# A fused attention and two-layer MoE kernel: a new order for the whole first phase, masks on VectorE, small steps on ScalarE, half-size weight checks

## The chip, the core and the metric

The kernel runs on one core of a Trainium2 chip. Its engines work from queues of their own, each in its order: TensorE (PE, with PEld for its weight loads), VectorE (DVE), ScalarE (ACT), GpSimd (POOL) and SyncE (SP), which issues the DMAs. The metric is the device time of one execution in microseconds (us).

## The reference

`x` is the output of a linear attention with a decaying state, for 4 batches, 8 heads, 768 positions and 48 features; then two dense layers follow, each on 3072 tokens of 384 features.

```python
for t in range(S):                                            # attention
    state = alpha[:, :, t, :, None] * state + np.einsum('bhd,bhe->bhde', k[:, :, t], v[:, :, t])
    y[:, :, t] = np.einsum('bhd,bhde->bhe', q[:, :, t], state)

h = x @ w_in                                                  # 384 -> 1024
e = np.exp(h - np.max(h, axis=-1, keepdims=True))
solu = h * (e / (np.sum(e, axis=-1, keepdims=True) + 1e-09))
mu = np.mean(solu, axis=-1, keepdims=True)
var = np.mean((solu - mu) ** 2, axis=-1, keepdims=True)
x = ((solu - mu) / np.sqrt(var + 1e-06) * g_ln) @ w_out       # 1024 -> 384

h = x @ w_in2                                                 # 384 -> 2048
out = (h * np.cos(h)) @ w_out2                                # 2048 -> 384
```

The weights arrive as 64-bit floats.

## The kernel before

**First phase.** The tokens are cut into 24 tiles of 128 (6 to a batch). For each tile the kernel runs an attention part and a first-layer part.

Attention of tile i: two scans over the decays with a floor and a reciprocal between them (`scan_to`, `total_floor`, `total_inverse`, `scan_from`; `S1` to `S4` in the list, all DVE), the scaling of keys and queries (`keys`, `queries`: `KR`, `QP` on POOL or `KV`, `QV` on DVE), a transposition of the keys (`TR`, PE) and its copy (`KT`, ACT), the scores (`SC`, PE, into PSUM tile `pa`), the causal mask into `am`, the state's product, addition and decay (`ST` PE, `SD` DVE, `SP` POOL or `SV` DVE), the values (`VA`, PE, into `px`), and their split into a high part `xh` (`XH`, ACT) and a low part `xl` (`XL`, DVE). The mask is made in one of two ways: `MV`, one DVE multiplication from PSUM, or `ME` and `MP`, a copy on ACT and a multiplication in place on POOL. The list has 7 tiles of the first kind and 17 of the second.

First layer of tile s: three products `HD s.0` to `HD s.2` (`hidden`, 18 matmuls of 512 columns in all, PE), the row maximum (`SM`, DVE), the exponential (`EX`, ACT), the guarded inverse (`O1`, `O2`), the product (`O3`) and the mean (`O4`, all DVE), the squares (`SQ`, ACT), three one-column steps on POOL (`PW`, `spread`), the normalisation (`NO`, ACT), its transposition in two halves (`TU`, PE), split into high and low parts (`TH` ACT, `TL` DVE). Every two tiles, three `project` groups of 24 matmuls (`PR`) give the columns of `x2T`, copied by ACT (`PX`). `ph`, the output of `hidden`, has one buffer, so that `HD s+1` waits for `O3` of tile s.

**Weights.** Each 64-bit block is read as pairs of integers and turned into a 32-bit float: a shift (`C1`, L206) and a sign step (`C2`, L210) on DVE, the low word on ACT (`CA`), the addition on POOL (`CD`) or DVE (`CV`). The 10 blocks of the first layer (`i0` to `i5`, `o0` to `o3`) are split into high and low parts (`WH` on ACT; `WL` on POOL or `WV` on DVE); the 16 blocks of the second layer are stored to a scratch in HBM (`WS`) and read again at the start of the second phase. `conv_load` (`CL`) has one buffer `raw` and three `top`.

**Order.** Every engine runs its instructions as they are issued, and they are issued in the order of one list, `PLAN`. Its head and tail are tables written out by hand (`START`, `END`); between them `_plan` makes one round for each tile from a template. A word of it is an operation and its tile or block: `HD4.0` is the first product of tile 4 (the fifth tile).

**Second phase.** 6 blocks of 512 tokens times 16 chunks of 128 hidden features make 96 slots. In slot t, PE runs `h2` of the chunk after and `out_mm` of the chunk two before (18 matmuls of 512 columns), ACT and DVE compute `h cos h` in between (`turns` L589, `residue` L595 and L596, `cosine` L602, `product` L607, `split_high` L612, `split_low` L617). At chunks 8 to 10 of a block, POOL makes a low part of the next block's input (`x2l`, L574). At the end of a block `out_end` copies and stores its three outputs. 42 slots from the 17th on also check the inputs: 18 blocks of `alpha` (`check`: POOL, then DVE L649) and 24 weight blocks of 128 x 768 (`check_weights`: a shift L657 and a comparison with a sum L658 on DVE, one buffer `wraw`), taking turns while there are both. A flag from them decides at the end whether a general path runs; it does not here.

Of the kernel before, what the change touches and what calls it, by code (L numbers as in the profile page):

```python
# [64 lines left out]
START = """  # L65
LP0 S10 CL0 S20 LP1 S30 S40 LQ0 CA0 QP0 C10 ID C20 S11 CL1 LQ1 S21 MK LV0 KV0 S31 TR0 C11 KT0 CL3 CD0 SC0 S41
ST0 KR1 CL2 C21 MV0 SD0 LP2 LV1 WH0 TR1 C13 C12 C23 QP1 C22 CA1 KT1 WL0 S12 CD1 VA0 SC1 S22 CL4
ME1 C14 LQ2 SV6 LV2 XH0 MP1 GL ST1 WH1 SD1 XL0 S32 WL1 C24 SP1 SP5 QP2 CA2 CA3 S42 CA4 CL5 LD3 CD3 CV2 CL6
C15 VA1 S13 S23 XH1 XL1 C25 HD0.0 KR2 TR2 SC2 S33 LD4 KT2 S43 ST2 QP3 MV2 WH3 CD4 VA2 WH2 KR3 SD2
TR3 CA5 WH4 SC3 XH2 CV5 C16 WL2 WL3 SP2 S14 C26 KT3 HD0.1 WH5 WL4 WL5 S24 ME3 S34 MP3 HD0.2 XL2  # L70
SM0 LD5 CA6 ST3 S44 QP4 SD3 EX0 VA3 O10 KR4 CL7 TR4 O20 XH3 O30 CD6 O40 XL3 SC4 SQ0 SP3 PW0 ME4 MP4 S15 C17 SV0
NO0 KT4 S25 QP5 C27 S35 HD1.0 CA7 WH6 HD1.1 HD1.2 ST4 LD6 S45 TU0.1 CD7 VA4 TH0.1 KR5 TU0.0 SM1 EX1 SD4 
O11 O21 O31 TR5 SP4 XH4 SC5 O41 S16 CL8 WH7 SQ1 TL0.1 HD2.0 WL6 PW1 ME5 HD2.1 C18 S26 S36 HD2.2 NO1 TU1.0 CA8 XL4 C28
S46 LD7 MP5 TH0.0 SM2 TL0.0 KR6 TH1.0 EX2 TU1.1 VA5 TR6 O12 TH1.1 QP6 XH5 KT6 O22 SC6 CD8 ME6 TL1.0 O32 LD8
S17 CL9 WL7 O42 TL1.1 WH8 XL5 MP6 HD3.0 S27 S37 S47 HD3.1 KR7 ST6 QP7 SD6 C19 S18 HD3.2 VA6 S28 C29 SQ2 S38 QV8
CA9 PW2 XH6 TR7 S48 KT7 LD9 SC7 ST7 SM3 NO2 KR8 SD7 TU2.1 TR8 SD5 ME7 XL6 SC8 EX3 TU2.0 CL10 O13 O23 CV9 KT8
O33 MP7 TH2.1 ST5 C110 VA7 HD4.0 TH2.0 HD4.1 TL2.1 WV8 WH9 O43 XH7 SP7 WV9 SQ3 TL2.0 HD4.2 PW3 LD10 C210 PR0.0 XL7
ST8 S19 MV8 CA10 NO3 S29 SD8 SP8 TU3.1 S39 S110 VA8 CL11 TH3.1 SM4 PX0.0 PR0.1 CD10 TU3.0 S210 EX4 TH3.0
TL3.1 S49 PX0.1 TL3.0 O14 O24 XH8 PR0.2 PX0.2 QP9 CA11 O34 O44 S310 SQ4 KR9 TR9 PW4 C111 KT9 SC9 HD5.0 HD5.1 C211
HD5.2 MV9 NO4 TU4.1 TH4.1 TU4.0 KT5 XL8 CD11 ST9 VA9 CL12 SM5 LD11 EX5 TL4.1 SD9 O15 TH4.0 TL4.0 PR1.0  # L80
S410 O25 KV10 O35 XH9 XL9 QP10 O45 PR1.1 SP9 S111 SQ5 TR10 PW5 SC10 WS10 S211 NO5 QP11 WS11 S311 MV10 S411 PX1.0 PX1.1
KT10 KR11 LD12 CA12 C112 C212 CD12 CL13 HD6.0 HD6.1 HD6.2 SM6 TU5.0 TU5.1 TH5.0 TL5.0 TH5.1 TL5.1 ST10 VA10
LD13 EX6 O16 O26 O36 O46 SD10 SP10 XH10 XL10 SQ6 PW6 PR1.2 PX1.2 PR2.0 PX2.0 PR2.1 PX2.1 TR11 SC11 NO6
"""
# [16 lines left out]


def _plan():

# [3 lines left out]
    start, end = table(START), table(END)  # L110
# [837 lines left out]
```

## Time and profile before

| | |
|---|---|
| median of 3 runs | 796.62 us (793.13 to 798.89) |
| profiled execution | 794.76 us, of which the span is 792.8 us |
| PE busy in the span | 741.8 us (94%) |
| DVE busy | 596.3 us (75%) |
| ACT busy | 404.7 us (51%) |
| POOL busy | 295.7 us (37%) |
| first phase, by the profile | 0 to about 380 us |

Times in the rows are counted from the start of the span. Busy time of PE includes matmuls that overlap. In a timeline, what stands in brackets at the end of a row is how long the engine was idle before it, and what ended that; neighbouring DVE instructions overlap by about 0.1 us.

### The profile page before, as it was taken

Reading aid. Unit: us, or ns where it says so; the run is one execution under the profiler, and the core shown is the slowest. Engines: PE = TensorE matmul, PEld = TensorE weight load, DVE = VectorE, ACT = ScalarE, POOL = GpSimd, SP = SyncE. Lnnn points to the kernel's source line nnn. Section 1 sums busy time; section 2 is a strip of 40 time slices with the busy share of each in tenths; the row PEclk is TensorE's granted clock in tenths of the full one; section 3 lists DMA queues with packets and bytes.
Section 4 is the critical chain, followed back from the end, with each engine's and each line's share of the span. In section 5 each row is a group of like instructions: output and inputs, shape, how many; then the busy total and the mean of one; then the engine's idle time right before and its main releaser. Section 6 shows DMA issues by size and latency. Waiting matters only on the chain.

```text
span 792.8 us, 13293 instructions
## 1 busy us (share of the span) xinstructions
PE 741.8 (94%) x5260; PEld 609.3 (77%) x5260; DVE 596.3 (75%) x937; ACT 404.7 (51%) x645; POOL 295.7 (37%) x229
## 2 busy tenths in 40 slices
PE   6587799999999999999999999999999899999997
PEld 3466588988888778979877787878787678888885
DVE  9998987677777696455567699979989876666664
ACT  3247544465566445556665454444444445545443
POOL 5789744567686732212454125123311100100000
PEclk9779999999999999999999999999999999999999
DMA  8734437556555542111221333243433411001001
GB/s 297 177 94 117 135 78 168 158 143 167 138 156 151 149 96 81 61 38 43 80 87 47 119 133 107 94 159 110 151 104 128 159 41 41 0 1 41 0 1 43
DMA packets 24502, 81.13 MB, mean 102 GB/s; under 512 B 3217, under 2 KB 6545, under 8 KB 24433
## 3 DMA queue, kind: packets, MB, share of 16 engines
q1 hardware_dynamic: 24432, 80.21, 33.6%
q8 instruction: 43, 0.70, 0.4%
q14 instruction: 27, 0.21, 0.1%
HBM read 69.19 MB, written 11.01 MB: 101 GB/s over the span
## 4 chain that ended last, share of the span: by engine, by line
PE 53%; DVE 25%; ACT 7%; DMA 7%; issue 5%; POOL 3%; ACTq 0%; SPq 0%; POOLq 0%; DVEq 0%
PE ph L423 10%; PE o L630 4%; PE h L582 4%; PE h L583 4%; PE h L584 4%; PE o L628 4%; PE o L629 4%; PE po L499 4%; DMA wraw<-w 4%; PE po L500 4%; PE po L501 4%; DVE r L596 3%; DVE r L595 3%; ACT g L602 3%; PE px L361 2%
## 5 line engine op out<-in xcount | busy, mean ns | idle before, releaser
L602 ACT ACTIVATE g<-r,halfpi 128x512 f32<-128x512 f32 x96 | 69.6, 725 | 146.7 <-DVE r L596 146.7
L630 PE MATMUL o<-gl,w2h 128*128 128x512 f32 x288 | 115.5, 401 | 10.0 <-DVE gl L617 9.9
L628 PE MATMUL o<-gh,w2h 128*128 128x512 f32 x288 | 113.8, 395 | 0.0
L582 PE MATMUL h<-x2h,w2h 128*128 128x512 f32 x288 | 113.7, 395 | 0.0
L583 PE MATMUL h<-x2l,w2h 128*128 128x512 f32 x288 | 113.5, 394 | 0.0
L629 PE MATMUL o<-gh,w2l 128*128 128x512 f32 x288 | 113.3, 393 | 0.0
L584 PE MATMUL h<-x2h,w2l 128*128 128x512 f32 x288 | 113.1, 393 | 0.0
L595 DVE SCALAR_TENSOR_TENSOR r<-n,h 128x512 f32<-128x512 int32 x96 | 65.8, 685 | 55.5 <-ACT n L589 55.5
L589 ACT ACTIVATE n<-h,quarter 128x512 int32<-128x512 f32 x96 | 65.7, 684 | 53.3 <-PE h L584 53.1
L607 DVE TENSOR_TENSOR g<-g,h 128x512 f32<-128x512 f32 x96 | 66.0, 688 | 31.3 <-ACT g L602 31.3
L499 PE MATMUL po<-lth,wout_h 128*128 128x256 f32 x288 | 82.4, 286 | 1.4 <-DVE ltl L492 1.0
L500 PE MATMUL po<-ltl,wout_h 128*128 128x256 f32 x288 | 80.7, 280 | 0.5 <-DVE ltl L492 0.5
L501 PE MATMUL po<-lth,wout_l 128*128 128x256 f32 x288 | 80.4, 279 | 0.0
L648 POOL TENSOR_SCALAR lim<-al 128x512 f32<-128x512 f32 x18 | 38.7, 2151 | 102.2 <-DMA al<-alpha 70.0
L630 PEld LDWEIGHTS o<-gl,w2h 128*128 128x128 f32 x288 | 54.0, 188 | 29.4 <-DVE gl L617 17.3
L596 DVE SCALAR_TENSOR_TENSOR r<-n,r 128x512 f32<-128x512 int32 x96 | 71.8, 748 | 3.3
L617 DVE TENSOR_TENSOR gl<-g,gh 128x512 fp32r<-128x512 f32 x96 | 67.6, 706 | 1.5 <-ACT gh L612 1.5
L429 DVE TENSOR_REDUCE c<-ph 128x1 f32<-128x1024 f32 x24 | 29.3, 1222 | 50.5 <-PE ph L423 46.4
L574 POOL TENSOR_TENSOR x2l<-x2T,x2h 128x512 fp32r<-128x512 f32 x15 | 19.4, 1296 | 119.8 <-ACT x2h L570 119.8
L582 PEld LDWEIGHTS h<-x2h,w2h 128*128 128x128 f32 x288 | 54.0, 188 | 12.7
L584 PEld LDWEIGHTS h<-x2h,w2l 128*128 128x128 f32 x288 | 54.1, 188 | 12.6
L629 PEld LDWEIGHTS o<-gh,w2l 128*128 128x128 f32 x288 | 54.0, 188 | 12.6
(116 smaller groups left out, 1605.3 us busy)
## 6 DMA issues: line engine op xcount, KB each, us to landing
raw<-w SPq DMA_DIRECT2D x16, 768.0 KB, 4.5
wraw<-w SPq DMA_DIRECT2D x16, 768.0 KB, 4.3
pk<-pack SPq DMA_DIRECT2D x42, 288.9 KB, 5.3
w2f<-top SPq DMA_DIRECT2D x16, 384.0 KB, 5.2
w2r<-w2f SPq DMA_DIRECT2D x16, 384.0 KB, 3.0
v<-vpack SPq DMA_DIRECT2D x24, 224.0 KB, 5.4
al<-alpha SPq DMA_DIRECT2D x18, 256.0 KB, 4.5
outT<-ob SPq DMA_DIRECT2D x18, 256.0 KB, 2.1
```

The lines of the kernel that those rows point to most:

```text
L499: PE.matmul(po, wout_h[:, k, fs], lh[:, k, :], start=k == 0, stop=False)
L500: PE.matmul(po, wout_h[:, k, fs], ll[:, k, :], start=False, stop=False)
L501: PE.matmul(po, wout_l[:, k, fs], lh[:, k, :], start=False, stop=k == NF1 - 1)
L582: PE.matmul(ph, wh[:, ks], xh[:, k, :], start=k == 0, stop=False)
L583: PE.matmul(ph, wh[:, ks], xl[:, k, :], start=False, stop=False)
L584: PE.matmul(ph, wl[:, ks], xh[:, k, :], start=False, stop=k == KT - 1)
L595: V.scalar_tensor_tensor(out=r, in0=n, scalar=-C1, in1=ph, op0=ALU.mult, op1=ALU.add)
L596: V.scalar_tensor_tensor(out=r, in0=n, scalar=-C2, in1=r, op0=ALU.mult, op1=ALU.add)
L602: A.activation(g, r, AF.Sin, bias=halfpi)
L628: PE.matmul(po, wh[:, fs], gh, start=c == 0, stop=False)
L629: PE.matmul(po, wl[:, fs], gh, start=False, stop=False)
L630: PE.matmul(po, wh[:, fs], gl, start=False, stop=c == NF2 - 1)
```

## The change

`PLAN` is written out as one table for the whole first phase; `START`, `END` and `_plan` are gone. In its words: all 24 masks are `MV` (DVE), and `ME`, `MP` do not exist any more. Keys are on DVE for 11 tiles (4 before), queries for 8 (2 before), the low parts of 5 weight blocks (2 before) and the additions of 8 (4 before). 8 state decays run on ACT (`SA`, four activations each), 8 on POOL, none on DVE. The guard and the mean have ACT versions (`A1` for 18 tiles, `A4` for 15). The three POOL steps of `spread` become one on ACT (`PA`), the power on POOL (`PW`) and one on ACT (`PB`). The memsets of states and constants move from DVE to POOL. `raw` has two buffers and `top` two. The weights are checked in 48 halves of 128 x 384 with two buffers, so that 66 slots hold a check.

```diff
-NWB = (KT * FF1 + NF1 * DM) // WB + NF2
+HB = WB // 2
+NWB = ((KT * FF1 + NF1 * DM) // WB + NF2) * 2
...
+PLAN = """
+LP0 GL CL0 MK LV0 ID LQ0 S10 LP1 S20 S30 S40 CA0 CL1 C10 C20 LV1 CD0 WH0 KV0 LQ1 WV0 TR0 LP2 S11 KT0 ST0 S21 S31 QP0
...
-                raw = cv.tile([128, WB, 2], I32, name=f"raw{name}", tag="raw", bufs=1)
-                tmp = [cv.tile([128, WB], I32, name=f"{t}{name}", tag=t, bufs=n) for t, n in (("top", 3), ("low", 1))]
+                raw = cv.tile([128, WB, 2], I32, name=f"raw{name}", tag="raw")
+                tmp = [cv.tile([128, WB], I32, name=f"{t}{name}", tag=t, bufs=n) for t, n in (("top", 2), ("low", 1))]
...
         def state_decay(i, eng=G):
             if 0 < i % NCH < NCH - 1:
                 P, st = T["P", i], T["st", i]
-                eng.tensor_tensor(st, st, P[:, :, C:C + 1].to_broadcast([128, NP, 96]), ALU.mult)
+                if eng is A:
+                    for p in range(NP):
+                        A.activation(st[:, p, :], st[:, p, :], AF.Copy, scale=P[:, p, C:C + 1])
+                else:
+                    eng.tensor_tensor(st, st, P[:, :, C:C + 1].to_broadcast([128, NP, 96]), ALU.mult)
...
+                A.activation(c[:, 1:2], c[:, 1:2], AF.Identity, bias=guards)
...
+                A.activation(c[:, 3:4], c[:, 3:4], AF.Copy, scale=-1.0 / FF1)
...
+        def variance(i):
+            c = T["c", i]
+            A.activation(c[:, 5:6], c[:, 4:5], AF.Identity, scale=1.0 / FF1, bias=tiny)
+
         def spread(i):
             c = T["c", i]
-            G.tensor_scalar(c[:, 5:6], c[:, 4:5], 1.0 / FF1, 1e-6, ALU.mult, ALU.add)
             G.tensor_tensor(c[:, 6:7], c[:, 5:6], mhalf, ALU.pow)
-            G.tensor_tensor(c[:, 7:8], c[:, 6:7], c[:, 3:4], ALU.mult)
+
+        def offset(i):
+            c = T["c", i]
+            A.activation(c[:, 7:8], c[:, 3:4], AF.Copy, scale=c[:, 6:7])
...
-            raw = pools["q3"].tile([128, WB, 2], I32, name=f"wraw{j}", tag="wraw", bufs=1)
-            y = pools["q3"].tile([128, WB], U32, name=f"wup{j}", tag="wup", bufs=1)
-            SP.dma_start(raw, weight_block(a, j).bitcast(I32).rearrange("p (n two) -> p n two", two=2))
+            raw = pools["q3"].tile([128, HB, 2], I32, name=f"wraw{j}", tag="wraw")
+            y = pools["q3"].tile([128, HB], U32, name=f"wup{j}", tag="wup", bufs=1)
+            src = weight_block(a, j // 2)[:, j % 2 * HB:(j % 2 + 1) * HB]
+            SP.dma_start(raw, src.bitcast(I32).rearrange("p (n two) -> p n two", two=2))
```

**Three places of the order.** On DVE at the start of the program, where `P` is the first scan's result, `pk` a tile's keys, queries and decays, `mage` and `magso` weight blocks in conversion and `am` a masked score; before:

```order
L277 SCALAR_TENSOR_TENSOR P_144<-pk_121,d1p 128x516
L282 TENSOR_SCALAR d1r_119<-P_144 128x4
L286 RECIPROCAL d1r_119<-d1r_119 128x4
L290 SCALAR_TENSOR_TENSOR pk_121<-pk_121,d1r_119 128x516
L206 TENSOR_SCALAR mage<-rawi_146 128x512
L210 SCALAR_TENSOR_TENSOR mage<-rawi_146,mage 128x512
L277 SCALAR_TENSOR_TENSOR P_158<-pk_122,d1p 128x516
L282 TENSOR_SCALAR d1r_120<-P_158 128x4
L298 TENSOR_TENSOR pk_121<-pk_121 128x512
```

and now:

```order
L254 SCALAR_TENSOR_TENSOR P_156<-pk_123,d1p 128x516
L259 TENSOR_SCALAR d1r_121<-P_156 128x4
L263 RECIPROCAL d1r_121<-d1r_121 128x4
L267 SCALAR_TENSOR_TENSOR pk_123<-pk_123,d1r_121 128x516
L183 TENSOR_SCALAR mage<-rawi_149 128x512
L187 SCALAR_TENSOR_TENSOR mage<-rawi_149,mage 128x512
L275 TENSOR_TENSOR pk_123<-pk_123 128x512
L216 TENSOR_TENSOR win_l<-mage,win_h 128x512
L254 SCALAR_TENSOR_TENSOR P_180<-pk_124,d1p 128x516
L259 TENSOR_SCALAR d1r_122<-P_180 128x4
```

The low part of the first weight block (L216, `WV0`) has come from POOL to DVE, and stands with the first tile's keys ahead of the second tile's first scan.

On POOL in the middle of the first phase, one round of the template before (`c` holds a tile's one-column values):

```order
L347 TENSOR_TENSOR am_2080<-am_2080,mask 128x1024
L298 TENSOR_TENSOR pk_121<-pk_121 128x512
L303 TENSOR_TENSOR pk_121<-pk_121,P_2084 128x512
L219 TENSOR_TENSOR top_1937<-top_1937,low_1938 128x768
L401 TENSOR_TENSOR S_124<-S_124,P_1925 128x384
L463 TENSOR_SCALAR c_2118<-c_2118 128x1
L464 TENSOR_TENSOR c_2118<-c_2118,mhalf 128x1
L465 TENSOR_TENSOR c_2118<-c_2118 128x1
```

and two tiles' worth of it now:

```order
L444 TENSOR_TENSOR c_2491<-c_2491,mhalf 128x1
L372 TENSOR_TENSOR S_126<-S_126,P_2346 128x384
L275 TENSOR_TENSOR pk_125<-pk_125 128x512
L280 TENSOR_TENSOR pk_123<-pk_123,P_2679 128x512
L444 TENSOR_TENSOR c_2610<-c_2610,mhalf 128x1
L196 TENSOR_TENSOR top_2429<-top_2429,low_2430 128x768
L444 TENSOR_TENSOR c_2790<-c_2790,mhalf 128x1
```

The mask and two of the three one-column steps are gone from POOL, and part of the keys, queries, additions and decays.

On DVE in the second phase, a slot with a weight check (`wup`), before:

```order
L595 SCALAR_TENSOR_TENSOR r_6_6183<-n_6_6178,h_3_6_6159 128x512
L596 SCALAR_TENSOR_TENSOR r_6_6183<-n_6_6178,r_6_6183 128x512
L617 TENSOR_TENSOR gl_5_6181<-g_5_6151,gh_5_6180 128x512
L607 TENSOR_TENSOR g_6_6187<-g_6_6187,h_3_6_6159 128x512
L657 TENSOR_SCALAR wup_6191<-wraw_6190 128x768
L658 SCALAR_TENSOR_TENSOR wup_6191,out<-wup_6191 128x768
```

and now, in the last block, where no check stood:

```order
L580 SCALAR_TENSOR_TENSOR r_4_7304<-n_4_7299,h_5_4_7280 128x512
L581 SCALAR_TENSOR_TENSOR r_4_7304<-n_4_7299,r_4_7304 128x512
L602 TENSOR_TENSOR gl_3_7302<-g_3_7272,gh_3_7301 128x512
L592 TENSOR_TENSOR g_4_7308<-g_4_7308,h_5_4_7280 128x512
L643 TENSOR_SCALAR wup_7312<-wraw_7311 128x384
L644 SCALAR_TENSOR_TENSOR wup_7312,out<-wup_7312 128x384
```

The check's place in its slot is the same; its width is half, and 24 slots more have one.

## Rows read from the trace of the kernel before

**Rows 1.** Busy us (count) per stretch: PE, PEld, DVE, ACT, POOL; clock, DMA share, GB/s.

```profile
0.00:60.00 60.00, 40.01 (x410) 28.64 (x410) 56.47 (x72) 19.92 (x31) 42.66 (x33) 0.83 0.64 188
60.00:99.00 39.00, 29.43 (x388) 22.56 (x387) 34.80 (x51) 26.64 (x43) 33.49 (x23) 0.96 0.49 127
99.00:268.00 169.00, 167.75 (x1834) 148.03 (x1833) 125.48 (x213) 92.68 (x151) 106.30 (x90) 1.00 0.54 147
268.00:382.00 114.00, 109.58 (x951) 96.25 (x950) 67.49 (x114) 64.76 (x106) 35.49 (x42) 1.00 0.22 65
...
450.00:647.00 197.00, 187.65 (x794) 147.39 (x793) 173.27 (x284) 91.32 (x146) 48.13 (x26) 1.00 0.36 125
647.00:777.00 130.00, 130.00 (x563) 105.02 (x562) 84.16 (x129) 63.71 (x101) 3.88 (x3) 1.00 0.04 13
```

**Rows 2.** Timeline of DVE, first 62 us: start us, duration us, instruction.

```profile
3.67 1.23 DVE L277 TENSOR_TENSOR_SCAN P<-pk,d1p 128x516 f32<-128x516 f32 x1 [0.21 <-DMA pk<-pack]
...
46.61 2.31 DVE L282 TENSOR_SCALAR d1r<-P 128x4 f32<-128x4 f32 x1
...
57.46 0.17 DVE L282 TENSOR_SCALAR d1r<-P 128x4 f32<-128x4 f32 x1
...
58.67 3.38 DVE L290 TENSOR_TENSOR_SCAN pk<-pk,d1r 128x516 f32<-128x516 f32 x1
61.97 1.19 DVE L429 TENSOR_REDUCE c<-ph 128x1 f32<-128x1024 f32 x1
```

**Rows 3.** Chain of work before the fifth tile's products; PE timeline at the 17th tile's.

```profile
76.54 10.24 DMA rawo<-wout
...
98.59 1.59 PE ph L423 x6
...
267.56 0.74 PE L423 MATMUL ph<-win_h,xh 128*128 128x512 f32 x2
```

**Rows 4.** Groups on DVE, 99 to 268 us: busy us, mean ns, idle before.

```profile
L336 DVE TENSOR_TENSOR am<-pa,mask 128x1024 f32<-128x1024 f32 x3 | 3.6, 1214 | 1.7 <-PE pa L320 1.7
...
L298 DVE TENSOR_TENSOR pk<-pk 128x512 f32<-128x512 f32 x1 | 0.7, 693 | 0.0
```

**Rows 5.** Groups on POOL, 0 to 380 us.

```profile
L347 POOL TENSOR_TENSOR am<-am,mask 128x1024 f32<-128x1024 f32 x17 | 43.3, 2545 | 30.8 <-ACT am L342 30.8
L303 POOL TENSOR_TENSOR pk<-pk,P 128x512 f32<-128x512 f32 x22 | 28.8, 1309 | 9.3 <-DMA pk<-pack 7.8 <-DMA v<-vpack 1.5
...
L219 POOL TENSOR_TENSOR mage<-mage,rawi 128x512 int32<-128x512 int32 x2 | 3.5, 1746 | 0.0
```

**Rows 6.** Timeline of ACT: `turns` of the 20th, 57th, 64th and 95th slot.

```profile
450.00 0.69 ACT L589 ACTIVATE n<-h,quarter 128x512 int32<-128x512 f32 x1 [1.19 <-PE h L584]
...
612.66 0.69 ACT L589 ACTIVATE n<-h,quarter 128x512 int32<-128x512 f32 x1 [0.38 <-PE h L584]
...
646.85 0.69 ACT L589 ACTIVATE n<-h,quarter 128x512 int32<-128x512 f32 x1 [0.99 <-PE h L584]
...
776.58 0.69 ACT L589 ACTIVATE n<-h,quarter 128x512 int32<-128x512 f32 x1 [1.22 <-PE h L584]
```

**Rows 7.** Timeline of POOL and DVE at three weight checks.

```profile
476.26 1.30 POOL L574 TENSOR_TENSOR x2l<-x2T,x2h 128x512 fp32r<-128x512 f32 x1 [8.48 <-ACT x2h L570]
476.29 1.68 DVE L657 TENSOR_SCALAR wup<-wraw 128x768 uint32<-128x768 uint32 x1
...
600.76 0.55 DVE L657 TENSOR_SCALAR wup<-wraw 128x768 uint32<-128x768 uint32 x1
601.35 0.96 DVE L658 SCALAR_TENSOR_TENSOR wup<-wup 128x768 f32<-128x768 uint32 x1
...
629.02 1.09 DVE L657 TENSOR_SCALAR wup<-wraw 128x768 uint32<-128x768 uint32 x1 [0.50 <-DMA wraw<-w]
```

**Rows 8.** DMA issues of the page: count, KB each, median us to landing.

```profile
wraw<-w SPq DMA_DIRECT2D x16, 768.0 KB, 4.3
...
w2r<-w2f SPq DMA_DIRECT2D x16, 384.0 KB, 3.0
```

More of the change, by code (lines that the diff above doesn't have):

```diff
@@ L62, in _feature_order @@
     return np.array(order)
[L65 to L80, printed above, removed]
@@ L729, in _build @@
                    GL=lambda: SP.dma_start(gln, a["gln"]), S1=scan_to, S2=total_floor, S3=total_inverse, S4=scan_from,
-                   C1=by_name(conv_shift), C2=by_name(conv_sign),
-                   CV=lambda n: conv_add(weights[n], V), WV=lambda n: split_rest(n, V), SV=lambda i: state_decay(i, V),
-                   O1=guard, O2=inverse, O3=solu, O4=mean,
-                   LD=load, CL=weights_load, KR=keys, KV=lambda i: keys(i, V), QP=queries,
-                   QV=lambda i: queries(i, V), TR=keys_turn, KT=keys_end, SC=scores, MV=causal, ME=scores_end,
@@ L735, in _build @@
-                   MP=scores_mask, ST=state, SD=state_add, SP=state_decay, VA=values, XH=values_high, XL=values_low,
-                   CA=by_name(conv_low), CD=by_name(conv_add),
-                   WH=split, WL=split_rest, WS=store, HD=hidden, SM=softmax, EX=expo, SQ=square, PW=spread,
-                   NO=norm, TU=turn, TH=turn_high, TL=turn_low, PR=project, PX=project_end, SB=second_first,
-                   XA=lambda k: xhigh(0, k), XS=lambda k: xlow(0, k, V), WD=w2load, WA=w2high, WG=w2low,
+                   C1=by_name(conv_shift), C2=by_name(conv_sign), CA=by_name(conv_low), CD=by_name(conv_add),
@@ new lines, in _build @@
+                   CV=lambda n: conv_add(weights[n], V), WH=split, WL=split_rest, WV=lambda n: split_rest(n, V), WS=store,
+                   CL=weights_load, LD=load, KR=keys, KV=lambda i: keys(i, V), QP=queries, QV=lambda i: queries(i, V),
+                   TR=keys_turn, KT=keys_end, SC=scores, MV=causal, ST=state, SD=state_add, SP=state_decay,
+                   SA=lambda i: state_decay(i, A), VA=values, XH=values_high, XL=values_low, HD=hidden, SM=softmax,
+                   EX=expo, O1=guard, A1=lambda i: guard(i, A), O2=inverse, O3=solu, O4=mean, A4=lambda i: mean(i, A),
@@ L740, in _build @@
+                   SQ=square, PA=variance, PW=spread, PB=offset, NO=norm, TU=turn, TH=turn_high, TL=turn_low,
+                   PR=project, PX=project_end, SB=second_first, XA=lambda k: xhigh(0, k), XS=lambda k: xlow(0, k, V),
+                   WD=w2load, WA=w2high, WG=w2low,
                    **{n: (lambda f: lambda c: once(f, 0, c))(f) for n, f in dict(
                        H2=h2, TN=turns, RS=residue, CS=cosine, CM=product, SH=split_high, SL=split_low).items()})
-        for op, *arg in PLAN:
-            OPS[op](*arg)
+        for word in PLAN.split():
+            OPS[word[:2]](*(int(x) for x in word[2:].split(".") if x))
@@ L814, in general @@
             n = KT * FF1 // WB
-            for j in range(NWB):
+            for j in range(NWB // 2):
                 dst = w2[:, j - 2 * n, :] if j >= 2 * n else \
```

134 lines of the change are left out of this document (65 added, 69 removed).

## The prediction

> **What bounds the kernel now.** I read the busy time by stretch first [rows 1]. It shows three regimes.
>
> From 0 to 99 us VectorE (DVE) is the bound: it is busy 56.47 + 34.80 = 91.3 of 99 us, while TensorE (PE) runs at a mean clock of 0.83 in the first 60 us, that is, it falls to its lower level between short bursts. GpSimd (POOL) is busy 76.2 us of these 99. The DVE timeline shows what the two do to each other [rows 2]: a scan takes 1.23 us at 3.67 and 3.38 us at 58.67; a four-column TENSOR_SCALAR takes 0.17 us at 57.46 and 2.31 us at 46.61; the reduction at 61.97, which reads PSUM, keeps its 1.19 us. So a good part of DVE's busy time here is waiting for POOL.
>
> From 99 to 382 us PE is the bound: busy 167.75 + 109.58 of 283 us, DVE only 74% and then 59% [rows 1].
>
> In the second phase a chunk (one *slot*) is paced by PE: 31 slots pass between the `turns` copies at 646.85 and 776.58, 4.185 us each [rows 6]. The 44 slots from 450.00 to 646.85 should have taken 184.1 us and took 196.9: 12.7 us are lost where the input checks run and DVE is busy 173 of 197 us [rows 1, 6]. 37 of these slots (to 612.66) lose 7.8 us, the last 7, which hold weight checks alone, lose 4.9.
>
> **The sum, against the profiled execution's 794.76 us** (the median of the runs shown is 796.62, 1.9 more).
>
> *A, up to the fifth tile's first product, at 98.59* [rows 3]. I counted the instructions that stand ahead of `HD4.0` in each list, each kind at its short, unstretched duration.
> - DVE: 68.7 us before, 78.1 us after. The 9.4 us more are 4 masks at 1.21 (4.9) and 12 multiplications and subtractions that were POOL's (four `KV`, three `QV`, five `WV`) at 0.69 and a little more for a wide one (8.5) [rows 4], less one forward and two backward scans at 1.23 (3.7) [rows 2]; the rest nearly cancels (three conversion steps more; state additions, low parts and one-column steps fewer).
> - POOL: 73.1 before, 39.5 after. 6 masks at 2.55 (15.3) and 10 keys and queries at up to 1.31 (12.7) go [rows 5]; the other 6 us are 4 splits, 2 decays and the one-column steps of 3 tiles off, two conversions and a wide split on, at their groups' means.
> - DVE's 91.3 busy us are 68.7 counted, about 2.5 of memsets at the start (now POOL's, but for the one of `d1p`) and so 20.1 of stretching; 7.7 are idle. If stretching goes with POOL's work it becomes 20.1 x 39.5/73.1 = 10.9.
> - A new wait: `WV0` stands on DVE third after the first conversion and needs POOL's addition (1.75) [rows 5] and then ScalarE's copy of the high part (under 0.7, as the 512-wide copies of [rows 6]); between stands only `KV0` (0.69). DVE waits about 1.7 us, and the second tile's scans stand behind it. The memsets give back at most the 0.21 us that the first scan waited for its DMA [rows 2].
> - The second `raw` buffer lets a weight load start earlier. The chain has one load of 10.24 us on it, at 76.54 [rows 3]; I allow 1 us for it, since DVE was working nearly all that time.
>
> Together 78.1 + 0.5 + 10.9 + 7.7 + 1.7 - 1 = 97.9 against 98.6: **-1**. Bounds: no stretching at all gives -11.6, the old 20.1 us gives +8.5. I take the proportional value, since the row that it is nearest to is the same mix of operations.
>
> *B, from there to the first steady slot at 382.* PE has nearly the same work behind this point in both lists (three groups of `project` have moved ahead of it, the attention products of two to four tiles behind it), so that only its waits can change: 1.25 us idle to 268 and 4.4 us to 382 [rows 1]. The new list keeps a piece of `project` for every gap of the last four tiles, so that I give 2 to 3 us of the 4.4 back. Up to `HD16.0` DVE's count grows from 131 to 153 us (11 masks, 8 keys and queries, 5 additions more) and POOL's falls from 115 to 51; DVE's 125.5 of 169 us become about 147. That is under PE's 168, but close: an in-order DVE at 87% answers PE late now and then, 0 to 2 us. ScalarE loses 17 copies and gets 113 small operations, each narrower than the 0.69 us of a 512-wide one [rows 6]: under 78 us on an engine busy 204 of 382 us [rows 1], so it hides them. **-2** (0 to -5.7, or later by rival 1).
>
> The Trainium skill ("ScalarE: Activation LUTs", What ACT_TABLE_LOAD costs) gives an activation with one pointer operand about 0.28 us plus 0.83 ns an element, so a decay in four pieces would be 1.4 us. No row here shows it; it would be within the bound above and change no term.
>
> *C, the checks.* A weight check is a shift of 0.55 us and a comparison of 0.96 us [rows 7]. With about 0.17 of each fixed, as the four-column instruction suggests [rows 2], a half block takes 0.36 + 0.56, near 0.9 us with overlap. DVE's other work in a slot is 84.16/31 = 2.7 us [rows 1], so such a slot needs 3.7 instead of 4.3 us, under PE's 4.185. With one buffer each load waited for the check before it (0.50 us idle and 1.09 instead of 0.55 us at 629.02), 768 KB landing in 4.3 us; a 384 KB load lands in 3.0 and there are two buffers [rows 7, 8].
> - The 7 weight-only slots: 4.9 lost, of which the three in which POOL's `x2l` meets the check keep about 1: gain 3.9.
> - The 37 mixed slots: 7.8 lost. The first check after a block's output waits for its load behind the output stores; a shorter load gains up to 2.5 us in two places. Where `x2l` (1.30 us at 476.26) meets a check, the shift takes 1.68 instead of 0.55 us [rows 7]; a half shift waits just as long for POOL, so only the shorter work is gained, 1 us. Together 3.4.
> - 24 checks more: they fill slots 63 to 86, among them three with `x2l` (3 x 1.1 us, less the 1.3 us that a slot has over) and two block ends: -1.3.
>
> **-6** (bounds -10 and 0). Sum -1 - 2 - 6 = -9: 785.8, or 787.6 from the median. I forecast 786.
>
> **Rivals.**
>
> 1. *DVE becomes the bound of the first phase (slower).* The list has DVE work of 231.4 us ahead of `HD16.0` (199.9 before), which begins at 267.56 now [rows 3]. If POOL's 90.4 us there stretch DVE as in the first 60 us, where 40.6 us counted on DVE and 43.8 on POOL (ahead of `HD1.0`) made 56.47 busy (0.36 us for each of POOL's), and DVE idles 7.8% as in the first 99 us, `HD16.0` begins at (231.9 + 32.8)/0.922 = 287: 20 us later, and with C the total is 809; at 0.275 us for each (the first 99 us) it begins at 278.5 and the total is 800. It decides from about 9 us of delay. For it: every key, split and mask now stands in DVE's one queue. Against: from 99 to 268 us DVE was stretched far less, with POOL busy 106 of 169 us, and PE had work to wait with. Price 803.
> 2. *The contention goes altogether.* Stretching falls on operations that read SBUF; masks read PSUM, as the unstretched reduction does [rows 2]. If what POOL keeps no longer meets them, A is -11.6 and B -3: 774. The Trainium skill ("SBUF — State Buffer", section "SBUF: two separate sides") states this as a lock held for a whole instruction, taken by GpSimd or by a DVE operation with two SBUF inputs or in a two-port mode, with the loser blocked fully; by that rule, and the trace agrees in its 0.17 against 2.31 us, meetings count and not a share of bandwidth. The same rule speaks against the new `KV`, `QV` and `WV`, which have two SBUF inputs.
> 3. *The new order changes nothing in sum*: A and B are 0, C as above: 789.
> 4. *Smaller checks give nothing*: DVE spends 48 x 0.9 = 43 instead of 24 x 1.5 = 36 us on them, meets `x2l` just as often, and the added slots lose what the old ones gain: 792.
>
> **How the numbers follow.** Forecast (780 to 790) 0.44, rival 3 0.18, rival 2 0.15, rival 1 0.13, rival 4 0.10. About 1% is what a measurement of this kernel can tell from no change, so faster means under 788.7: most of the forecast (0.34), rival 2 and a third of rival 3: 0.55. Slower means over 804.6: 0.10, of rival 1. The rest is 0.35. The range of 8 in 10 reaches into rivals 1 and 2: 771 to 801.
>
> **What would show it.** A: the start of the fifth tile's first `hidden` product (98.6 now), DVE's busy share to 99 us, and the mean length of the scans there. B: PE's idle time from 99 to 382 us, and whether PE waits for DVE's mask or low part. C: the time from the 20th to the 64th `turns` copy (196.9 now), and no DMA named ahead of the checks' shifts. I am wrong if PE, in the middle tiles, waits several us for DVE, or if the slots after 647 us lose more than 2 us.

## The result

The changed kernel takes 772.83 us (median of 4 runs, 771.5 to 775.41) beside 795.81 of the kernel before: a ratio of 0.9714, with a 95% interval of 0.9668 to 0.976. I had forecast 786 with a range of 771 to 801; the measured time lies just inside it. The direction was right and the size was not: 23 us instead of 10. The profiled executions differ by 21.1 us (773.7 and 794.76), and this is where they part.

| stretch | before, us | after, us | difference | forecast |
|---|---|---|---|---|
| A: start to `HD4.0` | 98.59 | 93.62 | -5.0 | -1 |
| B: from there to the 4th `turns` copy | 283.30 | 276.31 | -7.0 | -2 |
| C: 4th to 95th `turns` copy | 394.69 | 385.03 | -9.7 | -6 |
| rest | 18.18 | 18.74 | +0.6 | 0 |

The first row below is the 4th `turns` copy before; the other marks of before are in [rows 3, 6].

ACT timeline of the kernel before: start us, duration us, instruction.

```profile
381.89 0.69 ACT L589 ACTIVATE n<-h,quarter 128x512 int32<-128x512 f32 x1 [1.10 <-PE h L584]
```

The marks of the changed kernel: PE's timeline at `HD4.0` and at `HD16.0`, then ACT's at the 4th, 20th, 57th, 64th and 95th `turns` copy.

```profile
93.62 0.63 PE L394 MATMUL ph<-win_h,xh 128*128 128x512 f32 x2
...
258.43 0.63 PE L394 MATMUL ph<-win_h,xh 128*128 128x512 f32 x2
```

```profile
369.93 0.69 ACT L574 ACTIVATE n<-h,quarter 128x512 int32<-128x512 f32 x1 [1.70 <-PE h L569]
...
437.93 0.69 ACT L574 ACTIVATE n<-h,quarter 128x512 int32<-128x512 f32 x1 [1.20 <-PE h L569]
...
595.01 0.69 ACT L574 ACTIVATE n<-h,quarter 128x512 int32<-128x512 f32 x1 [1.21 <-PE h L569]
...
624.70 0.69 ACT L574 ACTIVATE n<-h,quarter 128x512 int32<-128x512 f32 x1 [0.96 <-PE h L569]
...
754.96 0.69 ACT L574 ACTIVATE n<-h,quarter 128x512 int32<-128x512 f32 x1 [1.21 <-PE h L569]
```

`HD16.0` starts 9.1 us earlier (258.43 against 267.56 in [rows 3]). The busy time by stretch of the changed kernel, cut at its own marks, answers [rows 1] (the columns are the same):

```profile
0.00:60.00 60.00, 39.23 (x390) 27.87 (x390) 50.88 (x72) 23.68 (x42) 26.31 (x29) 0.83 0.71 214
60.00:94.00 34.00, 29.23 (x298) 25.25 (x299) 31.83 (x48) 25.99 (x52) 13.80 (x10) 0.95 0.54 156
94.00:258.00 164.00, 163.58 (x1849) 141.97 (x1848) 152.62 (x222) 101.88 (x206) 55.79 (x43) 1.00 0.59 160
258.00:370.00 112.00, 112.00 (x1044) 100.33 (x1044) 62.79 (x103) 68.13 (x128) 24.60 (x22) 1.00 0.14 37
438.00:625.00 187.00, 184.47 (x795) 148.68 (x794) 159.49 (x289) 91.66 (x146) 44.33 (x26) 1.00 0.30 87
625.00:755.00 130.00, 129.68 (x561) 104.60 (x560) 105.43 (x197) 63.16 (x101) 3.89 (x3) 1.00 0.26 76
```

Three things are to be seen. To 94 us DVE is still the busiest engine (82.71 of 94), but with 40.1 us of POOL beside it instead of 76.2. From 94 to 370 us PE stands still for 0.42 us (1.25 + 4.42 before), although DVE is now 93% busy in the middle tiles. And 21 us of check work have moved into the stretch from 625 us, where DVE's 84.16 us became 105.43 and PE lost only 0.5 us. Every wait of PE for another engine from 93 to 258 us is one row:

```profile
PE ph L394 <- DVE so L423: 0.2, 1, 0.2
```

In the chain of work that ended last, PE's share has gone from 53 to 78% and DVE's from 25 to 14%.

### The profile page after: what moved, and what is told of

It is laid out like the page before. It is cut to its first block, busy times and chain, and to the rows that moved or that the text cites. A ratio compares the mean times of both kernels' runs of the same rounds, so it can differ in the third digit from the quotient of the medians.

```text
span 771.9 us, 13376 instructions
## 1 busy us (share of the span) xinstructions
PE 735.9 (95%) x5260; PEld 610.7 (79%) x5260; DVE 617.6 (80%) x1005; ACT 420.6 (54%) x741; POOL 193.8 (25%) x146
## 4 chain that ended last, share of the span: by engine, by line
PE 78%; DVE 14%; ACT 2%; issue 2%; DMA 2%; SPq 0%; POOL 0%; ACTq 0%; DVEq 0%; POOLq 0%
PE ph L394 12%; PE o L615 8%; PE h L567 7%; PE h L569 7%; PE h L568 7%; PE o L613 7%; PE o L614 7%; PE po L482 4%; PE po L483 4%; PE po L484 4%; PE px L328 4%; PE pl L461 3%; PE pa L297 2%; DVE r L580 1%; DVE P L254 1%
## 5 line engine op out<-in xcount | busy, mean ns | idle before, releaser
L581 DVE SCALAR_TENSOR_TENSOR r<-n,r 128x512 f32<-128x512 int32 x96 | 70.2, 731 | 3.3
L568 PEld LDWEIGHTS h<-x2l,w2h 128*128 128x128 f32 x288 | 54.2, 188 | 12.3
L613 PEld LDWEIGHTS o<-gh,w2h 128*128 128x128 f32 x288 | 54.1, 188 | 11.8
L597 ACT ACTIVATE gh<-g 128x512 fp32r<-128x512 f32 x96 | 59.8, 623 | 3.4 <-DVE g L592 3.1
## 6 DMA issues: line engine op xcount, KB each, us to landing
wraw<-w SPq DMA_DIRECT2D x32, 384.0 KB, 3.1
w2f<-top SPq DMA_DIRECT2D x16, 384.0 KB, 4.2
w2r<-w2f SPq DMA_DIRECT2D x16, 384.0 KB, 3.0
```

The source lines that it names most:

```text
L568: PE.matmul(ph, wh[:, ks], xl[:, k, :], start=False, stop=False)
L581: V.scalar_tensor_tensor(out=r, in0=n, scalar=-C2, in1=r, op0=ALU.mult, op1=ALU.add)
L613: PE.matmul(po, wh[:, fs], gh, start=c == 0, stop=False)
```

## The experiments

Ratios are to the kernel before, run beside it on the same chip; "phase 1" is the time to the 4th `turns` copy.

**1. The checks: size or buffer?**

```diff
-NWB = ((KT * FF1 + NF1 * DM) // WB + NF2) * 2
+NWB = (KT * FF1 + NF1 * DM) // WB + NF2
...
-            raw = pools["q3"].tile([128, HB, 2], I32, name=f"wraw{j}", tag="wraw")
+            raw = pools["q3"].tile([128, WB, 2], I32, name=f"wraw{j}", tag="wraw", bufs=1)
```

> The changed kernel with the weight checks of before (24 blocks of 128 x 768, one buffer); the first phase stays as changed. Theory (the checks' part is what the slots show): the slots from the 4th to the 95th took 394.7 us before and 385.0 in the changed kernel, so this one should give back 9.7 us, about 782.5, with the 7 weight-only slots again over 4.8 us each. Rival (the slots of the changed kernel are quicker for another reason, such as a second phase that starts with its data earlier): under 777.

Measured 783.75 (0.9842, 0.979 to 0.9893). The second kernel keeps the half-size checks and adds only `bufs=1` to `raw`:

> The changed kernel with half-size checks but one buffer for them. Theory (size matters, not the buffer): a half block lands in 3.1 us in the changed kernel, and with about 0.45 us to issue it this fits into a slot of 4.18 us beside the check before it, so at most 1.5 us are lost: 773 to 775, weight-only slots at 4.2 us. Rival (the second buffer is what counts): each of the 30 weight-only slots waits for its load, 4 us or more in sum: over 777.

Measured 773.03 (0.9704, 0.9649 to 0.9759). The third is the kernel before with the new checks (the diff above, read backwards):

> The kernel before with half-size, double-buffered weight checks and nothing else. If the checks are worth by themselves what they were worth in the changed kernel (783.75 with the old checks, 773 with the new: 10 to 11 us), this gives 785 to 786, its slots take about 385 us against 394.7, and the other 12 us belong to the first phase. If the checks gain only because the new first phase leaves the queues in another state, it stays at 790 or more. The forecast's own term was 6 us, which would give 790.

Measured 787.71 (0.99, 0.987 to 0.993). The 4th and the 95th `turns` copy of the three, in this order:

```profile
370.01 0.69 ACT L574 ACTIVATE n<-h,quarter 128x512 int32<-128x512 f32 x1 [1.72 <-PE h L569]
...
765.44 0.69 ACT L574 ACTIVATE n<-h,quarter 128x512 int32<-128x512 f32 x1 [1.19 <-PE h L569]
```

```profile
368.47 0.69 ACT L574 ACTIVATE n<-h,quarter 128x512 int32<-128x512 f32 x1 [1.70 <-PE h L569]
...
752.87 0.69 ACT L574 ACTIVATE n<-h,quarter 128x512 int32<-128x512 f32 x1 [1.21 <-PE h L569]
```

```profile
384.59 0.69 ACT L590 ACTIVATE n<-h,quarter 128x512 int32<-128x512 f32 x1 [1.11 <-PE h L585]
...
768.63 0.69 ACT L590 ACTIVATE n<-h,quarter 128x512 int32<-128x512 f32 x1 [1.20 <-PE h L585]
```

The slots take 395.4, 384.4 and 384.0 us (394.7 before, 385.0 after). So the checks gain 10 to 11 us in the slots whatever the first phase is, and the second buffer does nothing: what gains is that the checks are halves. A half is shorter, and half of the work moves to later slots; no run here separates the two. In the old first phase the whole time fell by 7 only, in the main since phase 1 of that profile was 2.7 us longer (384.59 against 381.89); all that I found beside it is a lower granted clock of PE (0.83 against 0.88 as the mean of the first 99 us).

**2. The order or the engines?** One kernel has the new list with every operation on the engine it had before; the other has the old list, with its buffers, and the new engines. Both have the new checks. The first lines of the lists that differ, against the changed kernel and against the kernel before:

```diff
-CA1 CL2 SD0 LV2 C11 SC0 C21 S41 LQ2 MV0 CD1 VA0 S12 WH1 CA2 CL3 C12 LD3 S22 XH0 C22 KV1 S32 CD2 TR1 XL0 KT1 S42
+CA1 CL2 SD0 LV2 C11 SC0 C21 S41 LQ2 MV0 CD1 VA0 S12 WH1 CA2 CL3 C12 LD3 S22 XH0 C22 KR1 S32 CV2 TR1 XL0 KT1 S42
-... SA1 QV1 QV2 SC1 WH3 S13 CL5 CA4 S23 MV1 WL2 S33 SC2
+... SP1 QP1 QP2 SC1 WH3 S13 CL5 CA4 S23 ME1 MP1 WL2 S33 SC2
```

> The changed kernel's order with the engines of before: masks of 17 tiles copied on ScalarE and multiplied on GpSimd, keys, queries, splits, additions, decays and one-column steps on the engines they had; half-size checks stay. Theory E (the engines make the first phase's gain, by freeing VectorE of the time it waits for GpSimd): the 12 us of the first phase come back, 783 to 787, VectorE stretched again by about 20 us in the first 95 us. Theory O (the order makes it): 773 to 777.

Measured 812.71 (1.0198, 1.014 to 1.0257).

```diff
-ST0 KR1 CL2 C21 MV0 SD0 LP2 LV1 WH0 TR1 C13 C12 C23 QP1 C22 CA1 KT1 WL0 S12 CD1 VA0 SC1 S22 CL4
-ME1 C14 LQ2 SV6 LV2 XH0 MP1 GL ST1
+ST0 KV1 CL2 C21 MV0 SD0 LP2 LV1 WH0 TR1 C13 C12 C23 QV1 C22 CA1 KT1 WV0 S12 CD1 VA0 SC1 S22 CL4
+MV1 C14 LQ2 LV2 XH0 GL ST1
```

> The order of before (its list, one raw buffer and three top buffers) with the engines of the changed kernel: all masks on VectorE, the same tiles' keys, queries, splits and additions moved, decays and one-column steps on ScalarE; half-size checks. Theory E (the engines make the gain): 773 to 777. Theory O (the order makes it): the first phase is as before, and only the checks' 9.7 us are gained: 785 to 788; where VectorE is loaded more without a fitting order, up to 792.

Measured 804.19 (1.009, 1.0057 to 1.0124). With the same checks in all four:

| | old engines | new engines |
|---|---|---|
| old order | 787.71 | 804.19 |
| new order | 812.71 | 772.83 |

Either step alone costs (25 and 16 us), both together gain 15. Both theories that I had set down fall: neither the list nor the engines hold the gain. What PE waits for in phase 1 differs in kind; first the new order with the old engines, then the old order with the new ones (sum us, times, longest):

```profile
PE px L338 <- POOL am L325: 9.8, 8, 2.8
PE pl L477 <- ACT so L469: 9.3, 6, 3.7
PE pkt L288 <- POOL pk L275: 7.2, 4, 4.3
PE px L338 <- POOL S L382: 5.1, 1, 5.1
```

```profile
PE po L484 <- DVE ltl L477: 14.2, 7, 3.2
PE ph L396 <- DVE so L425: 7.2, 5, 3.2
PE pkt L290 <- DVE pk L277: 6.3, 2, 3.6
PE ph L396 <- DVE win_l L218: 3.4, 2, 1.7
```

In the first PE is late for masks, keys and decays that POOL makes and for the normalised values (`so`) of ScalarE; in the second for low parts and products that stand on DVE behind work that the old list had put elsewhere, though DVE is far from full. The second kernel's busy time from 99 to 268 us (columns as in [rows 1]):

```profile
99.00:268.00 169.00, 154.15 (x1662) 135.59 (x1655) 129.84 (x188) 90.08 (x187) 42.00 (x35) 0.98 0.48 128
```

Not all of the loss is waiting. PE's own busy time in phase 1 is 356 us in both kernels and 344 us in the changed one, for the same matmuls, at a mean granted clock of 0.94 instead of 0.97. So of the 39 and 31 us that their phase 1 is longer, 12 are matmuls that take longer. That the waits bring the lower clock about is not shown.

**3. Which of the engine moves needs the new list?** In the changed kernel each group goes back to its old engines, at the same places: the 17 masks (`MVi` becomes `MEi MPi`), then keys, queries, low parts and additions (`KV`, `QV`, `WV` become `KR`, `QP`, `WL`), then the small steps and decays (`A1`, `A4`, `SA` become `O1`, `O4`, `SP`; `PA PW PB` one step on POOL).

> The changed kernel, with the masks of 17 tiles as before (a copy on ScalarE and a multiplication on GpSimd where the VectorE mask stood); all else as changed. VectorE has 17 x 1.21 = 21 us less to do, GpSimd 43 us more. Theory M (the masks are the largest part of what the old engines cost in the new order, since the mask lies on the path from the scores to the values and takes 1.0 + 2.5 us instead of 1.2): 785 to 795, TensorE waiting for GpSimd's am. Rival K (it is the keys, queries, splits and additions on GpSimd): under 780.

> The changed kernel, with keys, queries, low parts of the weights and additions on the engines of before (34 operations go from VectorE to GpSimd or back, most to GpSimd); masks and small steps as changed. Theory M: under 780. Rival K: 785 to 800, TensorE waiting for GpSimd's pk ahead of the turning of the keys and the scores.

> The changed kernel, with guard, mean and the three one-column steps on VectorE and GpSimd as before, and the decays on GpSimd or VectorE. Theories M and K both: at most 5 us lost, 773 to 778, since these steps are under 0.7 us each and off TensorE's path. A third theory (the normalisation's chain of three GpSimd steps is late for the turning): 780 to 790, TensorE waiting for so.

Measured 800.68 (1.0065, 1.0041 to 1.0089), 776.72 (0.9765, 0.9735 to 0.9795) and 776.11 (0.975, 0.9718 to 0.9782): the masks are worth 28 us in this list, the other two groups 4 and 3, which is within the intervals of the ratios and may be nothing. The reverse, all masks on DVE in the old list with everything else old but the checks:

```diff
-S12 CD1 VA0 SC1 S22 CL4 ME1 C14 LQ2 SV6 LV2 XH0 MP1 GL ST1
+S12 CD1 VA0 SC1 S22 CL4 MV1 C14 LQ2 SV6 LV2 XH0 GL ST1
```

> The order of before and its engines, but all 24 masks on VectorE in the place where the copies for them stood; half-size checks. Without the masks' change this would be about 786 (before less the checks' gain). If masks on VectorE are good by themselves (less waiting for GpSimd): 775 to 783. If they only pay in an order made for them, since in the old one they hold up what stands behind them on VectorE: 787 to 800.

Measured 788.7 (0.9909, 0.9885 to 0.9934), against 787.71 with the masks where they were: in the old list the move gives nothing, though it frees POOL of 43 us.

**4. Why do 17 masks cost 28 us there?** First only the load. A spare 128x384 tile is multiplied three times behind each of the 17 masks, which stay on DVE; then ScalarE has copies to make as well, four of a 128x64 tile at the same places. Nothing reads either.

```diff
+        def spare_mask(i):
+            for _ in range(4):
+                A.activation(copied, copied, AF.Copy)
+            for _ in range(3):
+                G.tensor_tensor(spare, spare, mask.unsqueeze(1).to_broadcast([128, 3, 128]), ALU.mult)
```

> The changed kernel with useless work on GpSimd: behind each of the 17 masks that used to be there, three multiplications of a spare 128x384 tile that nothing reads and that wait for nothing, about 2.8 us a mask and 47 us in all, so that GpSimd is about as busy in the first phase as with the masks. If GpSimd's work itself is what cost 28 us when the masks were given back to it (by stretching VectorE, at the 0.27 us per us of GpSimd that I took for the first 98 us 13 us, and by queueing ahead of its other steps), this takes 785 to 800. If the long way from scores to mask to values is what cost, GpSimd's load is nearly harmless and it takes 773 to 777.

> As e10 (useless multiplications on GpSimd behind 17 masks), and on ScalarE four useless copies of a spare 128x64 tile at the same places, about as long together as the copy of a mask (1.0 us), that nothing waits for. The masks themselves stay on VectorE. If the load on the two engines makes up the 28 us, 795 to 801. If ScalarE has room (102 of 164 us busy in the changed kernel's middle stretch) and the rest comes from the longer way from scores to values, 784 to 787, as in e10.

Measured 784.51 (0.9873, 0.9846 to 0.9899) with the multiplications alone and 784.62 (0.9844, 0.9804 to 0.9884) with both. The groups of the added work, and busy time of the first kernel to its 4th `turns` copy, then of the changed kernel to its own:

```profile
L325 POOL TENSOR_TENSOR spare<-spare,mask 128x384 f32<-128x384 f32 x51 | 60.8, 1192 | 2.8
...
0.00:379.00 379.00, 342.86 (x3575) 293.71 (x3576) 313.53 (x444) 219.37 (x424) 182.22 (x154) 0.97 0.46 128
```

```profile
L328 ACT ACTIVATE copied<-copied 128x64 f32<-128x64 f32 x68 | 17.3, 255 | 1.6
```

```profile
0.00:370.00 370.00, 344.03 (x3577) 295.42 (x3578) 298.13 (x443) 219.68 (x425) 120.50 (x103) 0.97 0.47 131
```

61.7 us more on POOL made the same work on DVE 15 us longer (313.53 less 298.13, less a memset of 0.4): 0.24 us for each. ScalarE's copies (17.3 us) cost nothing: it has room. In phase 1 the multiplications cost 9.4 us (379.3 against 369.9), and not through DVE alone: PE also waits 4.1 us for a decay in POOL's own queue. The same row of the kernel of 800.68 us, whose phase 1 is 27.2 us longer:

```profile
0.00:397.00 397.00, 352.94 (x3576) 300.04 (x3577) 292.84 (x426) 235.08 (x441) 163.48 (x120) 0.94 0.44 122
```

It shows the same stretch of DVE: 292.84 us, where 298.13 less 17 masks of 1.21 would be 277.5. But POOL has only 43 us more there (163.48 against 120.50) and not 62, so that the 9.4 us are at most what POOL's load makes of the 27, if masks act as the spare multiplications do. Another 9 us are PE's own matmuls: 352.94 us busy instead of 344.03, at a granted clock of 0.94 instead of 0.97, while the spare work left both as they were (342.86, 0.97). From 259 to 265 us the clock stood at its lower level (0.50), after PE had waited, and a `px` matmul took 0.42 us; from 267 to 273 us, at 1.00, it took 0.28.

Then the room. The copy and the multiplication stand right behind the scores, and the values step moves back towards the step that reads it.

> The changed kernel with 17 masks back on ScalarE and GpSimd as in the run of 800.7 us, but placed for it: the copy and the multiplication stand right behind the scores in the list, and the values step is moved back to just ahead of the step that reads it (18 to 45 places behind the scores instead of 10 to 24). If the 28 us came from an order that leaves a mask only the 1.2 us that VectorE takes, most of it comes back: 778 to 788. If they came from the work on the two engines, it stays at 796 to 802.

> As e11 (17 masks on ScalarE and GpSimd, begun right behind the scores), but the values step moves back only as far as the state it reads still stands: never past the next tile's state update. In e11 it was moved past that update, so that the state read was a later one and each values step waited for one more; its 840.6 us say nothing on the masks. If the rest of the 28 us (e10 gives some 12 of it to GpSimd's work alone) came from an order that leaves a mask too little time, 782 to 790. If the copies on ScalarE and the queues of the two engines are what cost, 796 to 802.

Measured 840.64 and 840.26. Both ran the same list: the limit that the second was meant to have moved nothing, so the state was not what was wrong. Some values steps stood behind the load that overwrites their tile's packed keys, queries and values, so in these two they work on a later tile's data and wait for it. They say nothing on the masks. The third has that mended (against the list of the kernel of 800.68 us):

```diff
-SC1 WH3 S13 CL5 CA4 S23 ME1 MP1 WL2 S33 SC2 C14 C24 VA1 QV3 CA5 CL6 C15 C25 XH1 LD4
+SC1 ME1 MP1 WH3 S13 CL5 CA4 S23 WL2 S33 SC2 C14 C24 QV3 CA5 CL6 C15 C25 VA1 XH1 LD4
```

> As e11 (17 masks on ScalarE and GpSimd, begun right behind the scores, the values step later), but no values step is moved behind the load that overwrites its tile's packed keys and values, three tiles on; in e11 (and e12, whose list came out the same) some were, so those values steps read the wrong tile and waited for its load. Mask and values step now stand 13 to 39 places apart instead of 4 to 23. If the 16 us that remain of the 28 come from an order that leaves a mask too little time, this takes 782 to 790; if they come from the copies and the queues of the two engines, 796 to 802.

Measured 826.57 (1.0395, 1.0339 to 1.0451): more room made it 26 us worse than the 800.68. The groups of copy and multiplication in phase 1, with the idle time ahead of them, at the old places and with room:

```profile
L327 POOL TENSOR_TENSOR am<-am,mask 128x1024 f32<-128x1024 f32 x17 | 42.5, 2501 | 73.8 <-ACT am L322 51.8 <-ACT c L444 19.2 <-PE ph L406 2.7
...
L322 ACT ACTIVATE am<-pa 128x1024 f32<-128x1024 f32 x17 | 17.4, 1024 | 10.4 <-PE pa L299 10.1 <-PE px L340 0.4
```

```profile
L327 POOL TENSOR_TENSOR am<-am,mask 128x1024 f32<-128x1024 f32 x17 | 41.9, 2466 | 103.3 <-ACT am L322 94.9 <-DVE S L374 8.5
...
L322 ACT ACTIVATE am<-pa 128x1024 f32<-128x1024 f32 x17 | 17.5, 1027 | 36.0 <-PE pa L299 26.7 <-PE px L340 9.3
```

PE's largest waits in phase 1 of the same two:

```profile
PE px L340 <- POOL am L327: 8.7, 7, 2.2
PE pkt L290 <- DVE pk L277: 7.2, 3, 4.2
PE pl L479 <- ACT so L471: 5.7, 3, 3.3
```

```profile
PE pl L479 <- ACT so L471: 18.6, 6, 4.9
PE ph L406 <- DVE so L435: 14.4, 8, 3.8
```

With room PE hardly waits for masks (0.8 us); it waits for ScalarE's and DVE's other steps. ScalarE's copies hold up its queue for 36 us, 27 of them for scores and 9 for the values step, since `am` has one buffer and a later values step holds it longer; POOL waits 95 us for ScalarE's copies, and what stands behind is late. So this run gives the masks more time and their buffer less, and doesn't test room alone. The same kind of wait is there, smaller, at the old places. That the other 18 of the 27 us, the 9 of longer matmuls among them, come from such waits at the head of two further queues is what these rows suggest; no run isolates it, so the cause of that part stays open.

**5. The keys' load.** The changed kernel with the first loads in another order:

```diff
-LP0 GL CL0 MK LV0 ID LQ0 S10
+LP0 LQ0 CL0 GL MK LV0 ID S10
```

> The changed kernel with the first steps of its list in another order: the loads of the first tile's keys and queries (LQ0) go out second, in front of the forget gates, the mask, the values and the identity. In the profile of the changed kernel VectorE idles 2.4 us near 10 us for this load. If that idle time is on the path to the first gate matmuls, as my forecast held of the first 98 us (whatever VectorE loses there delays the end), the time falls by 1 to 2.5 us, to 770.5 to 772, and the fifth tile's gate matmuls start at 91.5 to 92.5 instead of 93.6. If the stretch has slack elsewhere, or the values and the identity come late instead, it stays within 772.5 to 774.

Measured 772.5 (0.9716, 0.969 to 0.9741), the same as the changed kernel by this measurement, so the time decides nothing; the profiled span is 1.0 us shorter (770.9 against 771.9) and `HD4.0` 1.2 us earlier (92.4). DVE's timeline, the changed kernel first:

```profile
10.04 0.69 DVE L275 TENSOR_TENSOR pk<-pk 128x512 f32<-128x512 f32 x1 [2.44 <-DMA pk<-pack]
10.65 1.67 DVE L216 TENSOR_TENSOR win_l<-mage,win_h 128x512 fp32r<-128x512 f32 x1
```

```profile
8.19 0.68 DVE L276 TENSOR_TENSOR pk<-pk 128x512 f32<-128x512 f32 x1
10.69 0.99 DVE L217 TENSOR_TENSOR win_l<-mage,win_h 128x512 fp32r<-128x512 f32 x1 [1.82 <-ACT win_h L211]
```

With the load early, the next wait appears in its place: 1.82 us for the high part, the wait that the prediction had named for `WV0` (1.7).

## Why the prediction was right in direction and wrong in size

**A, the stretch of DVE: the term of 10.9 us was mis-sized.** Counted work came out as worked out: DVE's busy time to `HD4.0` is 82.3 us, of which 78.1 were counted and 0.5 is the memset, so 3.7 us are left where I had 10.9. Idle time is 11.3 instead of 9.4 us, and the raw buffer's 1 us is not seen as such. 78.1 + 0.5 + 3.7 + 11.3 = 93.6. The scans show the fall, before (to 99 us) and after (to 94 us), against 1.23 us unstretched; two more groups of after were still stretched, against 0.69 us (`pk`) and 0.55 (`topo`):

```profile
L290 DVE TENSOR_TENSOR_SCAN pk<-pk,d1r 128x516 f32<-128x516 f32 x9 | 17.0, 1884 | 0.1
L277 DVE TENSOR_TENSOR_SCAN P<-pk,d1p 128x516 f32<-128x516 f32 x9 | 14.2, 1577 | 1.6 <-POOL S L401 1.4 <-DMA pk<-pack 0.2
```

```profile
L267 DVE TENSOR_TENSOR_SCAN pk<-pk,d1r 128x516 f32<-128x516 f32 x8 | 11.3, 1408 | 0.0
L254 DVE TENSOR_TENSOR_SCAN P<-pk,d1p 128x516 f32<-128x516 f32 x8 | 10.7, 1342 | 2.0 <-DMA pk<-pack 2.0
...
L280 DVE TENSOR_TENSOR pk<-pk,P 128x512 f32<-128x512 f32 x4 | 3.9, 1004 | 0.0
...
L183 DVE TENSOR_SCALAR topo<-rawo 128x768 int32<-128x768 int32 x4 | 3.9, 981 | 0.0
```

The step that failed is the scaling of 20.1 us by POOL's counted work, 73.1 to 39.5. It has two faults. First, 20.1 and 3.7 are busy time less counted work, and neighbouring DVE instructions overlap: up to the mark their lengths add up to 96.4 us on 90.9 busy before, and to 88.4 on 82.3 after. So each remainder hides some 6 us of overlap, which does not shrink with POOL's work. By the lengths the stretch is about 25 us before (96.4 less 68.7 counted and 2.5 of memsets) and 10 after (88.4 less 78.1 and 0.5). Second, the stretch is not in proportion to POOL's time. It is 0.34 us per us of POOL to the mark before, 0.25 after, and 0.24 for the added multiplications of experiment 4; and from 99 to 382 us of the kernel before only about 10 us on 142 of POOL, 0.07. The row of the old mix did not carry over.

**The new wait** was real but masked: at 10.04 us DVE stands for the first keys' load, which I had not looked at, and by then `WV0`'s input is ready. Experiment 5 brings the forecast wait out.

**B: the term of -2 was mis-sized.** The place was right (PE's 1.25 and 4.4 us idle), but I gave back only 2 to 3 of the 5.7 us and took off up to 2 for a DVE at 87%. PE's idle time fell to 0.4 us, with DVE at 93%. The remaining 1.7 us of the 7.0 are PE's own busy time (277.3 before, 275.6 after), which I had taken as unchanged; it fell ahead of `HD4.0` too (69.4 to 68.5), and why is not shown.

The step that failed is that I priced the list (a gain) and DVE's load (a loss, by how busy it is) as two effects to be added. Experiment 2 shows that list and engines don't add: -15 together, +25 and +16 apart. A rate of DVE's occupation doesn't tell whether PE waits; the list with the new engines has 93% and no wait but 0.2 us, the old list with the same engines 77% (129.84 of 169 us from 99 to 268) and 14.2 us of waits for low parts, 13.6 of them in that stretch.

**C: mechanism right, size small.** The checks came out as priced, at 0.35 + 0.56 us, and where `x2l` meets one the shift still waits as long (1.47 us, so 1.1 more):

```profile
598.60 1.47 DVE L643 TENSOR_SCALAR wup<-wraw 128x384 uint32<-128x384 uint32 x1
600.11 0.56 DVE L644 SCALAR_TENSOR_TENSOR wup<-wup 128x384 f32<-128x384 uint32 x1
...
613.17 0.35 DVE L643 TENSOR_SCALAR wup<-wraw 128x384 uint32<-128x384 uint32 x1
613.56 0.56 DVE L644 SCALAR_TENSOR_TENSOR wup<-wup 128x384 f32<-128x384 uint32 x1
```

From the 20th to the 64th copy 186.8 us pass instead of 196.9: the 44 slots lose 2.6 us where I left 5.4. Most of that is the term of 3.4 us for the 37 mixed slots, which gained 5.6: they lose 2.2 us (to 595.01) instead of 7.8. The two loads behind a block's output, which I had at up to 2.5 us, gave back 1.9 (DVE waited 2.8 and 2.3 us for them, and now 1.2 and 2.0); the rest, by elimination, is the shorter work, for which I had 1 us. The 7 slots after them lose 0.4, where I left 1. The 31 slots after them take 130.26 instead of 129.73 us, so the 24 added checks cost 0.5, not 1.3. My reason for part of the gain, the second buffer that lets a load start earlier, was wrong: with one buffer the slots are as fast (experiment 1). A 384 KB load lands in 3.1 us (median of 32; 4.3 for 768 KB in [rows 8]), and that is soon enough but for four checks, whose shifts wait 0.7 to 2.2 us for their load. Half of the check work now lies in slots where DVE has room.

**The rivals.** DVE as the bound of the first phase (803) did not come: 231 us of DVE work ahead of `HD16.0` fitted into 258. (Its 0.36 us per us of POOL also took the 2.5 us of memsets for stretch; without them it is 0.31.) The old list with that work takes 804.19, near the price, but by another road: there DVE is 77% busy and PE waits for single results of it. The contention going altogether gave 774, near the time, but by other terms: A was -5 and not -11.6, since stretch and more idle time stay, and B and C were larger; that it came near is luck. By the rule of the Trainium skill that stood there ("SBUF — State Buffer", section "SBUF: two separate sides") meetings count and not a share of bandwidth. The trace agrees in so far as the stretch per us of POOL changed with the mix, 0.34, 0.25 and 0.07 in the three stretches above; and experiment 4 shows that stretching returns with POOL's work. That the order changes nothing (789) and that smaller checks give nothing (792) are both refuted, by experiments 2 and 1. Neither of the signs of being wrong that I had set came: PE waits 0.2 us in the middle tiles, and the slots after the 64th copy lose 0.5.

**The decays on ScalarE**, for which no row stood, are 4 pieces of 0.363 us:

```profile
L370 ACT ACTIVATE S<-S,P 128x96 f32<-128x96 f32 x32 | 9.3, 363 | 4.0 <-DVE S L362 3.9
```

That is 1.45 us a decay, on an engine with room. The Trainium skill's figure ("ScalarE: Activation LUTs", What ACT_TABLE_LOAD costs) had given an estimate of 1.4; the trace agrees.

## What to carry to other kernels

Where several in-order engines feed one another, an order and an assignment are one decision: price them together, by what each list leaves PE waiting for, and don't sum them as separate edits. Work that leaves a busy neighbour is worth more than its own length if the two stretch each other, but the rate of one mix doesn't hold for another; and read a stretch from the lengths of the instructions, since busy time less counted work hides their overlap. Smaller pieces of filler work gained here, by being shorter in full slots and by landing in slots with room, even though their number doubled.
